# RWKV channel mix behind induced attention, one core: stage B's maxima one step sooner, and the second batch's first block transposed on TensorE in the head

## The chip, the cores and the metric

The kernel runs on one core of a Trainium2 chip. The metric is the device time of one execution in microseconds (us). Engines are named as the profile has them: PE is TensorE's matmuls, PEld its weight loads, DVE is VectorE, ACT is ScalarE, POOL is GpSimd, and SPq is the DMA queue that SyncE feeds.

## The reference

x has 4 batches of 12608 tokens with 128 features; 32 inducing rows are given. The output of an induced attention goes through an RWKV channel mix:

```python
def mab(q, kv):
    s = scale * (q @ kv.transpose(0, 2, 1))
    s = s - s.max(-1, keepdims=True)
    a = np.exp(s)
    a /= a.sum(-1, keepdims=True) + 1e-09
    return a @ kv
h = mab(I, x)               # (4, 32, 128)
y = mab(x, h)               # (4, 12608, 128)
...
xk = mu_k * y + (1.0 - mu_k) * y_prev
xr = mu_r * y + (1.0 - mu_r) * y_prev
k = np.maximum(xk @ w_k, 0.0)     # w_k 128 x 1024
v = k * k @ w_v                   # w_v 1024 x 128
r = 1.0 / (1.0 + np.exp(-(xr @ w_r)))
return r * v
```

y_prev is y one token earlier (zero before the first). The weights arrive as 64-bit floats and are converted on the chip; all arithmetic is 32-bit.

## The kernel before, in words

**What is computed in place of the reference's steps.** A row of y is a mix of the 32 rows of h, so y is never formed. Stage A makes h of a batch, by blocks: scores of a block against the inducing rows (L391), running maximum (L394 to L414), exponentials, sums, and h accumulated (L458, L473). Stage B makes the softmax weights a of each token over the 32 rows of h, by blocks. The up projection then multiplies a tile R with tiles W0 and W1, which hold h times mu times w_k (and, in 128 columns more, w_r) for the token and for the token before. R has 128 rows: 32 rows of a in four copies, high and low parts in turn, so that W's high and low parts meet them in one matmul of 128 rows. The shift of one token is a shift of R's columns.

**Tiling.** A block is 2048 tokens (6 in a batch, and a tail of 320), a group is 512 tokens (25 in a batch, the last of 320), and a group has four units of 256 of the 1024 hidden columns. That makes 400 units, and the program is a loop of steps n, one for each unit. In step n, in this order:

- up(n): for two halves of 128 columns the matmuls L839 (R shifted forward, W0) and L841 (R, W1) into a PSUM tile ps_a, of which there are two;
- the events entered for this step by `soon`;
- in the second unit of a group, the gate's two matmuls L828 and L829, and the sigmoid L831 on ScalarE;
- the square: relu on VectorE (L851, called relu(n) here), the rounded square kh on ScalarE (L856), the full square on ScalarE (L857), and the rest kl = square - kh on GpSimd (L859). In the steps of the set `high_vector`, two in each block of 12 steps, kh is made on VectorE instead (L853, called kh(n)), which reads ps_a once more;
- down(n - 4): 6 matmuls L870, kh with w_v's high part, kh with its low part, kl with its high part;
- the events entered for this step by `at`.

When a group's last down projection is done, the gate product L875 and the transpose L886 follow on VectorE, and after every second group four stores L894 on SyncE's queue.

**What sets the order.** Every engine runs its instructions in the order in which the program issues them, and the order is written out by hand: `at(n, f)` and `soon(n, f)` put f into step n. Between the units stand, in segments of 12 steps (one block), stage A of the next batch and stage B of the next block of this one. With s the first step of a segment:

- stage A of batch b+1, `stage_a`: four transposes L359 on VectorE (`btr`) at s-3, s-1, s and s+3, each pair written to DRAM (L362, xd) and read back regrouped into xt (L365, `regroup`: two at s+1, two at s+5); the load of a later block (`load_x`, L207, 1 MB, and L200 for a tail) at s+5 behind the regroups; scores at s+13 and its maximum L394; the running maximum at s+14 (L403 to L414); exponentials at s+15; h at s+19; the accumulation L473 at s+20;
- stage B of block j+1, `stage_b`, at s+1 (the step in which stage A of the segment before has its scores): scores L649 into the PSUM tile pb_b; at the next step the transpose L656 and the maximum L659 (`trans`, `maxi`); then the subtraction L662 (`sub`), the exponential L666 on ScalarE, sum and reciprocal (L670 to L674), product and transpose back (L677, L683), high part L689 and low part L693, and the copies into R (L702, `spread`) by SyncE's queue.

All DMAs of these stages, the loads of x and the stores go through SyncE's one queue.

**The ends.** `head()` makes stage A of batch 0 (in four pieces u, v, w and the tail), converts the weights and starts W; `spin(n)` issues matmuls that only occupy TensorE. `hfin` (L528 to L550) turns h into hT and the factors h4k0, h4r0 and so on, h times mu. `start()` makes the first block of stage B in pieces (`sc`, `tu`, `df`, `ex`, `nm`, `hi`, `lo`, `put`: scores, transpose and maximum, difference L762, exponential L767, normalisation L774 to L777, high, low, copies into R L801 and L803), and W: `wpart` gives a product (L560), a high part (L563) and a low part (L566) for each of W0 and W1 and each of the two halves of the hidden columns (wa, wb) and the gate's columns (wg). The gate's first matmuls stand in step 4.

## Time and profile before

| | us |
|---|---|
| median of 3 runs | 1113.23 (1113.17 to 1113.67) |
| the profiled execution | 1114.14 |
| its span | 1111.9 |
| TensorE busy | 1088.7 |
| ScalarE busy | 966.5 |
| GpSimd busy | 951.7 |
| VectorE busy | 907.3 |

The span runs from the first to the last recorded instruction. Busy time counts instructions at work; a matmul's end is modelled, so an interval between two starts says more than a row's length. In the waits a row reads "engine, what waited, its line <- engine, what it waited for, its line: total us, count, longest". In a timeline a row has its start, its length, engine, line, operation, output <- input, tile and count, and in brackets the idle time ahead of it and what ended it. In windows a row has the stretch, its length, the busy us of PE, PEld, DVE, ACT and POOL with counts, the granted clock of TensorE, the DMA engines' busy share, and GB/s.

### The profile page before, as it was taken

The page shows a single profiled execution, that of the slowest core. Times are in us where ns is not written, and L with a number is a line of the kernel's source. Part 1 is how long each engine was busy: PE and PEld are TensorE (multiplying, and loading weights), DVE is VectorE, ACT ScalarE, POOL GpSimd, SP SyncE. Part 2 cuts the span into 40 slices and gives each one's busy share as a digit, 9 for nine tenths or more (in the row PEclk, how much of TensorE's full clock was granted, in tenths as well). Part 3 has the DMA queues.
Part 4 walks back from the last instruction along what each step waited for, and adds up shares of the span by engine and source line. Part 5 has one row for each costly group of instructions (what it writes and reads, how often), then busy time and mean ns, then how long its engine had stood idle before and what let it go on. Part 6 is the DMA issues. An engine that isn't in the chain of part 4 may idle for free.

```text
span 1111.9 us, 17188 instructions
## 1 busy us (share of the span) xinstructions
PE 1088.7 (98%) x5723; PEld 832.8 (75%) x5723; DVE 907.3 (82%) x1287; ACT 966.5 (87%) x1098; POOL 951.7 (86%) x417
## 2 busy tenths in 40 slices
PE   8899999999999999999999999999999999999997
PEld 6577777777777777777787777777777787777886
DVE  6988888986878899887778888888676888887665
ACT  6698889889889888888898988979889998999995
POOL 3388998898898988889888999879898899999997
PEclk9999999999999999999999999999999999999999
DMA  9045655661356556653235646655223132232212
GB/s 343 10 127 120 171 147 145 155 167 25 62 135 150 154 148 152 146 152 82 48 78 151 167 119 149 160 138 133 41 55 73 36 66 58 55 70 57 45 29 35
DMA packets 256247, 121.10 MB, mean 109 GB/s; under 512 B 221440, under 2 KB 224672, under 8 KB 253856
## 3 DMA queue, kind: packets, MB, share of 16 engines
q1 hardware_dynamic: 255152, 119.92, 45.2%
q8 instruction: 45, 0.74, 0.3%
q14 instruction: 42, 0.34, 0.1%
q10 hardware_dynamic: 1008, 0.10, 0.1%
HBM read 46.94 MB, written 44.70 MB: 82 GB/s over the span
## 4 chain that ended last, share of the span: by engine, by line
PE 71%; DVE 13%; ACT 4%; issue 3%; DMA 2%; POOL 0%; SPq 0%; DVEq 0%; ACTq 0%; POOLq 0%
PE ps_v L870 35%; PE ps_a L839 14%; PE ps_a L841 13%; DVE k_t L851 6%; PE pb_b L649 2%; ACT kh L856 2%; DVE kh L853 2%; PE pb_a L458 2%; PE pb_a L391 2%; PE ps_v L828 2%; PE ps_v L829 2%; DMA R<-R 1%; DVE s L656 1%; DVE oT L875 1%; ACT k_t L857 1%
## 5 line engine op out<-in xcount | busy, mean ns | idle before, releaser
L859 POOL TENSOR_TENSOR kl<-k_t,kh 128x1024 fp32r<-128x1024 f32 (+1 forms) x399 | 937.3, 2384 | 122.1 <-ACT k_t L857 101.0
L851 DVE TENSOR_SCALAR k_t<-ps_a 128x1024 f32<-128x1024 f32 (+1 forms) x400 | 479.1, 1198 | 142.0 <-PE ps_a L841 115.9
L857 ACT ACTIVATE k_t<-k_t 128x1024 f32<-128x1024 f32 (+1 forms) x400 | 418.4, 1048 | 34.1 <-DVE kh L853 23.0
L856 ACT ACTIVATE kh<-k_t 128x1024 fp32r<-128x1024 f32 (+1 forms) x352 | 365.2, 1038 | 82.7 <-PE ps_v L870 41.6
L839 PE MATMUL ps_a<-R,W 128*128 128x512 f32 (+1 forms) x800 | 323.5, 405 | 8.6 <-DVE k_t L851 4.5
L841 PE MATMUL ps_a<-R,W 128*128 128x512 f32 (+1 forms) x800 | 313.5, 392 | 0.0
L870 PE MATMUL ps_v<-kh,wvh 128*128 128x512 f32 (+1 forms) x800 | 248.4, 391 | 0.0
L870 PE MATMUL ps_v<-kl,wvh 128*128 128x512 f32 (+1 forms) x800 | 247.3, 390 | 0.9 <-POOL kl L859 0.3
L870 PE MATMUL ps_v<-kh,wvl 128*128 128x512 f32 (+1 forms) x800 | 246.8, 390 | 0.0
L839 PEld LDWEIGHTS ps_a<-R,W 128*128 128x128 f32 x800 | 150.8, 188 | 76.7 <-DVE kh L853 10.6
L870 PEld LDWEIGHTS ps_v<-kl,wvh 128*128 128x128 f32 x800 | 148.1, 188 | 38.2 <-POOL kl L859 6.9
L870 PEld LDWEIGHTS ps_v<-kh,wvh 128*128 128x128 f32 x800 | 149.6, 188 | 34.2
L870 PEld LDWEIGHTS ps_v<-kh,wvl 128*128 128x128 f32 x800 | 149.6, 188 | 34.1
L841 PEld LDWEIGHTS ps_a<-R,W 128*128 128x128 f32 x800 | 150.4, 188 | 30.6 <-issue 0.2
L875 DVE TENSOR_TENSOR oT<-ps_v,rT 128x512 f32<-128x512 f32 (+1 forms) x100 | 66.6, 666 | 1.8
L886 DVE STREAM_TRANSPOSE ot<-oT 128x512 f32<-128x512 f32 x96 | 67.2, 700 | 0.0
L853 DVE SCALAR_TENSOR_TENSOR kh<-ps_a,k_t 128x1024 fp32r<-128x1024 f32 x48 | 58.8, 1224 | 5.0
L359 DVE STREAM_TRANSPOSE xs<-xb 128x512 f32<-128x512 f32 x72 | 50.0, 694 | 11.7 <-DMA xb<-in_x_dram 11.7
L831 ACT ACTIVATE rT<-ps_v 128x512 f32<-128x512 f32 (+1 forms) x99 | 57.8, 584 | 0.3
L831 ACT ACT_TABLE_LOAD x31 | 39.8, 1283 | 0.5
L828 PE MATMUL ps_v<-R,W 128*128 128x512 f32 (+1 forms) x99 | 39.1, 395 | 0.4 <-DVE oT L875 0.4
L829 PE MATMUL ps_v<-R,W 128*128 128x512 f32 (+1 forms) x99 | 38.9, 393 | 0.0
(217 smaller groups left out, 607.7 us busy)
## 6 DMA issues: line engine op xcount, KB each, us to landing
out_dram<-ot SPq DMA_DIRECT2D x184, 128.0 KB, 3.3
xb<-in_x_dram SPq DMA_DIRECT2D x18, 1024.0 KB, 6.8
xd<-xs SPq DMA_DIRECT2D x36, 512.0 KB, 3.1
xt<-xd SPq DMA_DIRECT2D x72, 256.0 KB, 4.2
R<-ah SPq DMA_DIRECT2D x184, 64.0 KB, 2.1
R<-al SPq DMA_DIRECT2D x184, 64.0 KB, 2.1
kl<-in_x_dram SPq DMA_DIRECT2D x4, 512.0 KB, 8.8
xb<-in_x_dram SPq DMA_DIRECT2D x4, 512.0 KB, 11.1
```

The costliest lines, as they stand in the source:

```text
L828: nc.tensor.matmul(out=ps[:, :w], lhsT=S.W[0][:, F:WF], rhs=R[:, 1:w + 1], start=True, stop=False)
L831: nc.scalar.activation(out=self.rT, in_=ps[:, :w], func=AF.Sigmoid)
L839: nc.tensor.matmul(out=ps[:, c, :w], lhsT=S.W[0][:, cs], rhs=R[:, 1:w + 1], start=True, stop=False)
L841: nc.tensor.matmul(out=ps[:, c, :w], lhsT=S.W[1][:, cs], rhs=R[:, 0:w], start=False, stop=True)
L851: nc.vector.tensor_scalar(out=k, in0=self.ps[:, :, :w], scalar1=0.0, scalar2=None, op0=ALU.max)
L853: nc.vector.scalar_tensor_tensor(out=kh, in0=self.ps[:, :, :w], scalar=0.0, in1=k, op0=ALU.max, op1=ALU.mult)
L856: nc.scalar.activation(out=kh, in_=k, func=AF.Square)
L857: nc.scalar.activation(out=k, in_=k, func=AF.Square)
L859: return lambda eng, a, z: eng.tensor_tensor(out=kl[:, :, a:z], in0=k[:, :, a:z], in1=kh.bitcast(F32)[:, :, a:z], op=ALU.subtract)
L870: nc.tensor.matmul(out=self.v, lhsT=wt[:, fc, :], rhs=kk[:, c, :], start=(fc == 0 and n == 0), stop=(fc == FC - 1 and n == 2))
L875: nc.vector.tensor_tensor(out=self.oT, in0=self.v, in1=self.rT, op=ALU.mult)
L886: nc.vector.transpose(out=ot[:, o:o + w], in_=self.oT)
```

## The change

**Stage B.** `trans` and `maxi` are entered for the step of the scores instead of the next, `sub` for the next. In the variant for a batch's very first stages (`quick`) the same, and the sums, the product and the copies one step later. In stage A the first transpose moves from s-3 to s-2 and the accumulation from s+20 to s+21.

In VectorE's order around one block's stage-A maximum (step 29 and the steps behind it; mx is stage A's maximum, s stage B's transposed scores, mkr the running maximum, k_t a unit's relu) there stood before:

```order
L394 TENSOR_REDUCE mx_1539<-pb_a 128x1
L851 TENSOR_SCALAR k_t<-ps_a 128x1024
L403 TENSOR_SCALAR mh<-mx_1539 64x1
L406 TENSOR_SCALAR mkr<-mh,mkr 32x1
L413 COPY mkr<-mkr 32x1
L414 COPY mkr<-mkr 64x1
L656 STREAM_TRANSPOSE s_1580<-pb_b 128x512
L659 TENSOR_REDUCE pb_b<-s_1580 128x16
L851 TENSOR_SCALAR k_t<-ps_a 128x1024
L359 STREAM_TRANSPOSE xs<-xb 128x512
L662 TENSOR_TENSOR s_1580<-s_1580,pb_b 128x512
L875 TENSOR_TENSOR oT<-ps_v,rT 128x512
```

and now (L664, L667 and L670 are the transpose, the maximum and the subtraction, L859 the relu):

```order
L402 TENSOR_REDUCE mx_1540<-pb_a 128x1
L664 STREAM_TRANSPOSE s_1553<-pb_b 128x512
L667 TENSOR_REDUCE pb_b<-s_1553 128x16
L859 TENSOR_SCALAR k_t<-ps_a 128x1024
L411 TENSOR_SCALAR mh<-mx_1540 64x1
L414 TENSOR_SCALAR mkr<-mh,mkr 32x1
L421 COPY mkr<-mkr 32x1
L422 COPY mkr<-mkr 64x1
L670 TENSOR_TENSOR s_1553<-s_1553,pb_b 128x512
L859 TENSOR_SCALAR k_t<-ps_a 128x1024
L364 STREAM_TRANSPOSE xs<-xb 128x512
L883 TENSOR_TENSOR oT<-ps_v,rT 128x512
```

The transpose and the maximum stand ahead of the first relu, and the subtraction ahead of the second.

**Loads and stores.** `load_x` is entered ahead of the regroups of its step, and the stores of a pair of groups are sent two steps after the transpose (`send`), but for the last two groups of all. On SyncE's queue at the first load of another batch (xd and xt are the two sides of the regrouping, xb and xl the loads, R<-R a single column carried on) there stood before:

```order
L362 DMA xd<-xs 128x1024
L894 DMA out_dram<-ot 32x32x32 x4
L365 DMA xt<-xd 32x4x512 x2
L207 DMA xb<-in_x_dram 128x2048
L200 DMA xl<-in_x_dram 80x4x128
L628 DMA R<-R 128x1
```

and now:

```order
L367 DMA xd<-xs 128x1024
L212 DMA xb<-in_x_dram 128x2048
L205 DMA xl<-in_x_dram 80x4x128
L370 DMA xt<-xd 32x4x512 x2
L905 DMA out_dram<-ot 32x32x32 x4
L636 DMA R<-R 128x1
```

The load has moved past four stores and two regroups.

**Batch 1's first block.** `ahead_of_time()` is new. Sixteen transposes on TensorE in the head take the place of seven spin matmuls; four copies on ScalarE put the result into the two W tiles of batch 1, which are still free; the scores are made in step 2, copied to SBUF in step 3, and two transfers inside SBUF bring the block home to xt. The four transposes L359, the transfers by xd, and the scores in step 17 are gone for this block.

**The start.** The split of w_v into high and low parts moves from the head to behind the second piece's exponential; the later steps of w_r's conversion move between the first pieces; the gate's factors h4r are made on GpSimd from SBUF, h4k0 is made from SBUF; the gate's weights are multiplied in step 2 instead of 1, and their high and low parts made in step 3 instead of 1. In VectorE's order in the first steps (W with 64x128 are the gate's low parts, the rows behind s and pb_b the third piece of stage B) there stood before:

```order
L851 TENSOR_SCALAR k_t<-ps_a 128x1024
L359 STREAM_TRANSPOSE xs<-xb 128x512
L566 TENSOR_TENSOR W_677<-ps_v,W_677 64x128
L566 TENSOR_TENSOR W_678<-ps_v,W_678 64x128
L851 TENSOR_SCALAR k_t<-ps_a 128x1024
L756 STREAM_TRANSPOSE s_811<-pb_b 128x256
L757 TENSOR_REDUCE pb_b<-s_811 128x8
L762 TENSOR_TENSOR s_811<-s_811,pb_b 128x256
L851 TENSOR_SCALAR k_t<-ps_a 128x1024
L359 STREAM_TRANSPOSE xs<-xb 128x512
L774 TENSOR_REDUCE pb_b<-s_811 128x8
```

and now:

```order
L859 TENSOR_SCALAR k_t<-ps_a 128x1024 x2
L764 STREAM_TRANSPOSE s_823<-pb_b 128x256
L765 TENSOR_REDUCE pb_b<-s_823 128x8
L770 TENSOR_TENSOR s_823<-s_823,pb_b 128x256
L859 TENSOR_SCALAR k_t<-ps_a 128x1024
L782 TENSOR_REDUCE pb_b<-s_823 128x8
L783 TENSOR_SCALAR sm_842<-pb_b 128x8
L784 RECIPROCAL pb_b<-sm_842 128x8
L785 TENSOR_TENSOR pb_b<-s_823,pb_b 128x256
L574 TENSOR_TENSOR W_683<-ps_v,W_683 64x128
L574 TENSOR_TENSOR W_684<-ps_v,W_684 64x128
```

The gate's low parts now stand behind the third piece's normalisation, and the transposes of batch 1 are gone.

**The end.** The last unit's kl, which VectorE makes, is issued two steps later, behind the gate and the transpose of the group before the last.

The diff, cut to what the text speaks of:

```diff
         def scores():
-            ps = pb_tile("a")
+            if sooner:
+                ps = S.s1
+            else:
+                ps = pb_tile("a")
             L["s1"] = ps
-            for i in range(Q):
+            for i in range(0 if sooner else Q):
                 nc.tensor.matmul(out=ps[M * i:M * (i + 1), :], lhsT=indT, rhs=S.xt[j, i],
...
-        for c in range(Q):
-            at(t + (-3, -1, 0, 3)[c], lambda c=c: btr(c))
+        k = order_a.index((b, j))
+        for bn, jn in order_a[k + 1:]:
+            if jn < NBLK - 1:
+                at(t + 5, lambda: load_x(bn, jn))
+                if jn == NBLK - 2:
+                    at(t + 5, lambda: load_x(bn, jt))
+                break
+        for c in range(0 if sooner else Q):
+            at(t + (-2, -1, 0, 3)[c], lambda c=c: btr(c))
             at(t + (1, 1, 5, 5)[c], lambda c=c: regroup(c))
...
         at(t + 19, t_hmm)
-        at(t + 20, acc)
-        k = order_a.index((b, j))
-        for bn, jn in order_a[k + 1:]:
-            if jn < NBLK - 1:
-                at(t + 5, lambda: load_x(bn, jn))
-                if jn == NBLK - 2:
-                    at(t + 5, lambda: load_x(bn, jt))
-                break
+        at(t + 21, acc)
...
                     h4 = L["h4"][nm] = sm.tile([P, P], F32, name="h4" + nm, bufs=1)
-                    nc.scalar.activation(out=h4, in_=L["hp"], func=AF.Copy, scale=mu)
+                    nc.gpsimd.tensor_tensor(out=h4, in0=L["h"], in1=mu.broadcast_to([P, P]), op=ALU.mult)
                 else:
...
             S.hT = h[:, :M]
-            L["hp"] = ps[:, :P]
+            L["hp"], L["h"] = ps[:, :P], h
             L["h4"] = {}
...
                 h4 = L["h4"]["k0"] = sm.tile([P, P], F32, name="h4k0", bufs=1)
-                nc.scalar.activation(out=h4, in_=L["hp"], func=AF.Copy, scale=muk)
+                nc.scalar.activation(out=h4, in_=h, func=AF.Copy, scale=muk)
             else:
...
             at(t, scores)
-            for n, f in ((1, trans), (1, maxi), (1, sub), (2, total), (2, recip), (3, mult), (3, back), (4, low)):
+            for n, f in ((0, trans), (0, maxi), (1, sub), (3, total), (3, recip), (4, mult), (4, back), (5, low)):
                 at(t + n, f)
             soon(t + 2, expo)
-            soon(t + 4, high)
+            soon(t + 5, high)
             for i in range(Q):
-                at(t + 5 + i, lambda i=i: spread(i))
+                at(t + 6 + i, lambda i=i: spread(i))
             return
         at(t, scores)
-        at(t + 1, trans)
-        at(t + 1, maxi)
-        at(t + 2, sub)
+        at(t, trans)
+        at(t, maxi)
+        at(t + 1, sub)
         at(t + 3, expo)
...
                 dst = out[self.b, t0:t0 + o - o0 + w, :].rearrange("(s q) (j d) -> j q s d", q=M, d=M)
-                for i in range(Q):
-                    eng = nc.scalar if self.b == B - 1 and g == NG - 1 and i % 2 else nc.sync
-                    eng.dma_start(out=dst[i], in_=ot[M * i:M * (i + 1), o0:o + w]
-                                      .rearrange("q (s d) -> q s d", d=M))
+                final = self.b == B - 1 and g == NG - 1
+                def send():
+                    for i in range(Q):
+                        eng = nc.scalar if final and i % 2 else nc.sync
+                        eng.dma_start(out=dst[i], in_=ot[M * i:M * (i + 1), o0:o + w]
+                                          .rearrange("q (s d) -> q s d", d=M))
+                if self.b == B - 1 and g >= NG - 2:
+                    send()
+                else:
+                    at(n + 2, send)
...
+    def ahead_of_time():
+        S = batches[1]
+        T = [wp.tile([P, WF], F32, name=f"W{s}")[:, :2 * G].rearrange("c (i g) -> c i g", i=2) for s in range(2)]
+        X = {"n": 0, "ps": {}}
+        for i in range(Q):
+            S.xt[0, i] = T[i // 2][:, i % 2]
+        def turn(n):
+            for _ in range(n):
+                k = X["n"]
+                X["n"] += 1
+                h, s = divmod(k, 2 * Q)
+                if s == 0:
+                    X["ps"][h] = pa.tile([P, 2, G], F32, name="ps_a")
+                nc.tensor.transpose(out=X["ps"][h][:, s // Q, (s % Q) * P:(s % Q + 1) * P],
+                                    in_=S.xb[0][:, k, :], identity=ident)
+        def keep(h, k):
+            src = X["ps"][h].rearrange("c a n -> c (a n)").rearrange("c (s i q) -> c i s q", i=Q, q=M)
+            nc.scalar.copy(out=T[k][:, :, h * G // 2:(h + 1) * G // 2].rearrange("c i (s q) -> c i s q", q=M),
+                           in_=src[:, 2 * k:2 * k + 2])
+        def scores():
+            X["s"] = pv.tile([P, G], F32, name="ps_v")
+            for i in range(Q):
+                nc.tensor.matmul(out=X["s"][M * i:M * (i + 1), :], lhsT=indT, rhs=S.xt[0, i],
+                                 start=True, stop=True)
+        def settle():
+            S.s1 = st.tile([P, G], F32, name="e1t", bufs=1)
+            nc.scalar.copy(out=S.s1, in_=X["s"])
+        def home():
+            S.xtb[0] = xt_pool.tile([P, Q, G], F32, name="xt")
+            for k in range(2):
+                nc.sync.dma_start(out=S.xtb[0][:, 2 * k:2 * k + 2, :], in_=T[k])
+            for i in range(Q):
+                S.xt[0, i] = S.xtb[0][:, i, :]
+        return turn, keep, scores, settle, home
+    sooner = ahead_of_time()
     def head():
...
         S = batches[0]
+        turn, keep = sooner[:2]
         work = [conv["k", 0], conv["k", 1], conv["v", 0], conv["v", 1], []]
...
         w.expo()
-        for c in range(FC // cg):
-            split_wv(c)
-        spin(5)
+        turn(10)
+        keep(0, 0)
+        keep(0, 1)
         v.etrans()
...
         weights()
+        turn(2)
         w.hmm(1)
         w.acc()
-        run(conv["r", 0][:2])
-        spin(2)
+        turn(4)
+        keep(1, 0)
+        keep(1, 1)
         hfin()
...
         S = batches[0]
-        run([gates, sc0, sc1, tu0, df0, ex0, wa[0][0], wa[1][0], wb[0][0], lambda: spin(2), tu1, nm0, *conv["r", 0][2:], wa[0][1], hi0,
-             wa[1][1], wb[0][1], lo0, wa[0][2], put0, lambda: spin(2),
-             df1, ex1, wa[1][2], nm1, hi1])
-        for n, f in ((0, wb[1][0]), (0, wb[1][1]), (1, lambda: run([w[0] for w in wg])),
-                     (1, sc2), (1, put1)):
+        whigh, wlow = zip(*[split_wv(c) for c in range(FC // cg)])
+        scores_1, settle_1, home_1 = sooner[2:]
+        rexp, rman, rsign, rjoin = conv["r", 0]
+        run([sc0, gates, rexp, sc1, tu0, df0, ex0, wa[0][0], wa[1][0], wb[0][0], lambda: spin(2), tu1, nm0, wa[0][1],
+             hi0, rman, rsign, wa[1][1], wb[0][1], lo0, put0, lambda: spin(2), wa[0][2], wa[1][2], df1, rjoin, ex1,
+             *whigh, *wlow, nm1, hi1])
+        for n, f in ((0, wb[1][0]), (0, wb[1][1]), (1, sc2), (1, put1), (2, lambda: run([w[0] for w in wg])), (2, scores_1)):
             soon(n, f)
-        for n, f in ((0, lo1), (0, wb[0][2]), (0, wb[1][2]), (2, tu2), (2, df2), (2, ex2), (3, nm2)):
+        for n, f in ((0, wb[0][2]), (0, wb[1][2]), (0, lo1),
+                     (2, tu2), (2, df2), (2, ex2), (3, nm2)):
             at(n, f)
         for prod, high, low in wg:
-            soon(1, high)
-            at(1, low)
+            soon(3, high)
+            at(3, low)
+        at(3, settle_1)
+        at(3, home_1)
         for k, (high, low, put) in enumerate(pl1):
...
                 low = grp.square(u, n in high_vector)
-                low(nc.vector if n == end else nc.gpsimd, 0, grp.w)
+                if n < end:
+                    low(nc.gpsimd, 0, grp.w)
             if 1 <= m <= len(units) and units[m - 1][1] == NU - 1:
-                units[m - 1][0].store()
+                units[m - 1][0].store(n)
+            if n == end + 2:
+                low(nc.vector, 0, units[end][0].w)
             if old is not None:
```

More of the change, by code (lines that the diff above doesn't have):

```diff
@@ L168, in split_wv, with high, low @@
         cs = slice(c * cg, (c + 1) * cg)
-        nc.scalar.copy(out=wvh[:, cs, :], in_=wv_sb[:, cs, :])
-        nc.gpsimd.tensor_tensor(out=wvl[:, cs, :], in0=wv_sb[:, cs, :], in1=wvh.bitcast(F32)[:, cs, :],
-                                op=ALU.subtract)
+        def high():
+            nc.scalar.copy(out=wvh[:, cs, :], in_=wv_sb[:, cs, :])
+        def low():
+            nc.gpsimd.tensor_tensor(out=wvl[:, cs, :], in0=wv_sb[:, cs, :], in1=wvh.bitcast(F32)[:, cs, :],
+                                    op=ALU.subtract)
+        return high, low
     def groups(j):
@@ L348, in stage_a @@
         tw = TAIL // Q
-        last = 4 if tail else 0
+        sooner = b == 1 and j == 0
         def btr(c):
@@ L416, in expo @@
         def expo():
-            e1t = st.tile([P, G], F32, name="e1t", bufs=1)
+            e1t = S.s1 if sooner else st.tile([P, G], F32, name="e1t", bufs=1)
             if j == 0:
@@ L875, in gate, with store @@
             nc.vector.tensor_tensor(out=self.oT, in0=self.v, in1=self.rT, op=ALU.mult)
-        def store(self):
+        def store(self, n):
             g, w = self.g, self.w
```

## The prediction

> **What bounds the kernel now.** I read the busy shares first, then the waits, then TensorE's and VectorE's timelines around the waits that repeat. In the busy shares each engine has its busy us, its share of the span and its instructions:
>
> ```profile
> span 1111.9 us, 17188 instructions
> PE 1088.7 (98%) x5723; PEld 832.8 (75%) x5723; DVE 907.3 (82%) x1287; ACT 966.5 (87%) x1098; POOL 951.7 (86%) x417
> ```
>
> TensorE bounds: 98% busy. The change removes hardly any matmul, so what can be won is time in which TensorE stands still or starts late, and a gain elsewhere that ends no such wait counts nothing. The view of waits gives, for each group, total us, count and longest:
>
> ```profile
> PEld ps_a L839 <- DVE kh L853: 10.6, 16, 0.8
> ```
>
> Sixteen weight loads of an up projection wait for the rounded square on VectorE. One of them in TensorE's timeline (start, length; the bracket is idle time with modelled ends, so I go by distances of starts):
>
> ```profile
> 92.38 1.06 PE L391 MATMUL pb_a<-xt,indT 128*32 128x512 f32 x8
> 93.27 1.04 PE L649 MATMUL pb_b<-xt,hT 128*32 128x512 f32 x8
> ...
> 98.51 0.62 PE L870 MATMUL ps_v<-kl,wvh 128*128 128x512 f32 x2
> 98.96 0.40 PE L839 MATMUL ps_a<-R,W 128*128 128x512 f32 x1
> 99.19 0.41 PE L841 MATMUL ps_a<-R,W 128*128 128x512 f32 x1
> ...
> 103.63 0.62 PE L870 MATMUL ps_v<-kl,wvh 128*128 128x512 f32 x2
> 104.50 0.49 PE L839 MATMUL ps_a<-R,W 128*128 128x512 f32 x1 [0.24 <-DVE kh L853]
> 104.83 0.39 PE L841 MATMUL ps_a<-R,W 128*128 128x512 f32 x1
> ```
>
> Up(20) follows the last pair of its predecessor by 98.96 − 98.51 = 0.45 us and its second matmul by 0.23. Up(22) follows by 0.87 and 0.33. The place loses 0.42 + 0.10 = 0.52 us. On VectorE, up to there:
>
> ```profile
> 93.52 0.69 DVE L394 TENSOR_REDUCE mx<-pb_a 128x1 f32<-128x512 f32 x1 [0.96 <-PE pb_a L391]
> 95.55 1.22 DVE L851 TENSOR_SCALAR k_t<-ps_a 128x1024 f32<-128x1024 f32 x1 [1.34 <-PE ps_a L841]
> ...
> 97.62 0.72 DVE L656 STREAM_TRANSPOSE s<-pb_b 128x512 f32<-128x512 f32 x1
> 98.37 0.69 DVE L659 TENSOR_REDUCE pb_b<-s 128x16 f32<-128x512 f32 x1
> 98.98 1.21 DVE L851 TENSOR_SCALAR k_t<-ps_a 128x1024 f32<-128x1024 f32 x1
> ...
> 100.73 0.65 DVE L662 TENSOR_TENSOR s<-s,pb_b 128x512 f32<-128x512 f32 x1
> ...
> 103.22 1.22 DVE L853 SCALAR_TENSOR_TENSOR kh<-ps_a,k_t 128x1024 fp32r<-128x1024 f32 x1
> ```
>
> VectorE idles 1.34 us at step 18 and is late five instructions later: from 95.55 on it runs almost without a gap to kh's end at 104.44, just ahead of the delayed matmul.
>
> **Part 1, stage B's maxima.** Transpose and maxima (L656, L659) go ahead of relu(18). Their scores end at 93.27 + 1.04 = 94.31; the pair takes 98.98 − 97.62 = 1.36, so relu(18) starts at about 95.75 where it started at 95.55: 0.2 to 0.3 later. From behind it 1.36 us vanish. So kh(20) ends at about 104.44 − 1.36 + 0.25 = 103.35, or, with starts rounded up on the way, 103.65. Undelayed, up(22) wants it at 103.63 + 0.45 = 104.08. So 0.4 to 0.7 us are to spare and the 0.52 goes away. Going through TensorE's timeline I count this wait, at this place of a block, 14 times (the other two of the 16 stand in the start and at a late load): 14 × 0.52 = **−7.3 us**. Next late is nothing: relu(18) must have left its PSUM tile by up(20) at 98.96 and ends at 97.05, 1.9 early. The last stage of batch 0 has a related wait, on VectorE for the exponentials, and TensorE behind it:
>
> ```profile
> 298.85 0.69 DVE L670 TENSOR_REDUCE pb_b<-s 128x16 f32<-128x512 f32 x1 [0.83 <-ACT s L666]
> ```
> ```profile
> 299.87 0.40 PE L841 MATMUL ps_a<-R,W 128*128 128x512 f32 x1
> 300.69 0.50 PE L828 MATMUL ps_v<-R,W 128*128 128x512 f32 x1 [0.42 <-DVE oT L875]
> ```
>
> The subtraction comes a step sooner and so do the exponentials' inputs: 0.82 − 0.23 + 0.10, **−0.7 us**; between 0 and that, since the exponentials' own place on ScalarE is unchanged.
>
> **Part 2, the load ahead of the regroups.** On SyncE's queue at a new batch, and what waited:
>
> ```profile
> 458.77 0.34 SPq L362 DMA_DIRECT2D xd<-xs  x1
> 464.15 3.89 SPq L894 DMA_DIRECT2D out_dram<-ot  x4
> 469.30 0.38 SPq L207 DMA_DIRECT2D xb<-in_x_dram  x1
> ```
> ```profile
> 477.91 0.71 DVE L359 STREAM_TRANSPOSE xs<-xb 128x512 f32<-128x512 f32 x1 [3.31 <-DMA xb<-in_x_dram]
> ```
> ```profile
> 477.62 0.62 PE L870 MATMUL ps_v<-kl,wvh 128*128 128x512 f32 x2
> 479.79 0.50 PE L839 MATMUL ps_a<-R,W 128*128 128x512 f32 x1 [1.54 <-DVE k_t L851]
> ```
>
> The transpose needs a load that was issued behind the stores. TensorE loses 2.17 − 0.45 = 1.72. In the new order the load follows xd directly, so issue moves from 469.30 to about 460, and the block's first transpose stands one step later. The wait was 3.31 and the move is 9 us: it goes entirely. The other late load, one batch on, costs about 1.3 by the same reading; with 0.1 each for the following matmul, **−3.1 us** (at least −2, if stores two steps later delay something else by some tenths).
>
> **Part 3, the start.** Batch 1's first block is transposed on TensorE in place of spin matmuls, so its scores leave step 17: the eight L391 above took 93.27 − 92.38 = 0.89. Against this stands the gate's weights. Before:
>
> ```profile
> 54.67 0.40 PE L828 MATMUL pb_a<-R,W 128*128 128x512 f32 x1
> ```
> ```profile
> 55.60 0.40 ACT L767 ACTIVATE s<-s 128x256 f32<-128x256 f32 x1
> ```
> ```profile
> 56.47 0.39 DVE L774 TENSOR_REDUCE pb_b<-s 128x8 f32<-128x256 f32 x1
> 57.34 0.43 DVE L777 TENSOR_TENSOR pb_b<-s,pb_b 128x256 f32<-128x256 f32 x1
> ```
>
> Now the gate's low weights stand on VectorE behind the third piece's normalisation, and that behind the exponential, which is itself behind the squares. From 56.00 the normalisation takes 57.77 − 56.47 = 1.30, the two lows a quarter each by their size: the gate matmul at 57.4 to 57.7 instead of 54.67, **+2.7**. What was waiting just behind in the batch is then no longer late:
>
> ```profile
> 71.88 0.50 PE L839 MATMUL ps_a<-R,W 128*128 128x512 f32 x1
> 77.24 0.47 PE L839 MATMUL ps_a<-R,W 128*128 128x512 f32 x1 [0.43 <-DVE k_t L851]
> ```
>
> These two are late by 0.3 and 0.6 by their distances, and the transposes of batch 1 that VectorE ran there are gone. With 0.9 from step 17 and 0.2 to 0.5 from up(0) starting sooner (its converters and the gate factors leave the chain ahead), 2.7 − 0.9 − 0.9 − 0.4 = **+0.5**, bounds −1.0 (up(0) a whole microsecond sooner, with the gate behind it) and +2.5 (nothing repaid but some tenths). The four copies run on ScalarE while TensorE still has spin or weight work, and the two transfers inside the chip are wanted only in step 23: nothing. The split of w_v, moved behind the first piece of stage B, is first read by down(0), which stands behind the same delayed gate matmul: nothing; if it is later than that, down(0) is late by the difference.
>
> **Part 4, the end.** VectorE's last instructions and SyncE's last issue:
>
> ```profile
> 1102.47 2.10 DVE L859 TENSOR_TENSOR kl<-k_t,kh 128x640 fp32r<-128x640 f32 x1 [1.64 <-ACT k_t L857]
> 1104.49 0.68 DVE L875 TENSOR_TENSOR oT<-ps_v,rT 128x512 f32<-128x512 f32 x1
> 1106.02 0.49 DVE L875 TENSOR_TENSOR oT<-ps_v,rT 128x320 f32<-128x320 f32 x1
> ```
> ```profile
> 1107.99 1.10 SPq L894 DMA_DIRECT2D out_dram<-aT  x2
> ```
>
> The gate of group 23 and its transpose (0.68 + 0.7) fit into the 1.64 before kl. The last gate then waits for the last matmul, and the stores of group 23 are out of the way of the last: **−1.2**, bounds −0.4 (only the last gate moves) and −1.6.
>
> **Sum.** −7.3 − 0.7 − 3.1 + 0.5 − 1.2 = −11.8. The profiled execution took 1114.14 us, 0.91 above the median of the runs shown; on that median 1113.23 − 11.8 = **1101.4 us**.
>
> **The clock as a rule against part 3.** The last matmul, and the granted clock behind it (the fraction stands last but two):
>
> ```profile
> 1104.93 0.45 PE L870 MATMUL ps_v<-kl,wvh 128*128 128x320 f32 x2
> ```
> ```profile
> 1108.00:1109.00 1.00, 0.00 (x0) 0.00 (x0) 0.00 (x0) 0.00 (x0) 0.00 (x0) 0.83 0.99 142
> 1109.00:1111.00 2.00, 0.00 (x0) 0.00 (x0) 0.00 (x0) 0.00 (x0) 0.00 (x0) 0.50 0.51 71
> ```
>
> The mean of 0.83 puts the fall to 0.50 at two thirds of that microsecond, 3.3 us after the last matmul's end. The idle time ahead of the delayed gate matmul is up to 57.7 − 54.7 = 3.0 us, close to it. The Trainium skill, TensorE: Matmul & The Clock Gate, part 1, says the same: after about 3.4 us of idle window the clock is halved until a window as long has been busy, with windows that run free. This trace agrees at its end; whether the start crosses the line no row of before can show.
>
> **Rivals.**
> - *The maxima start late.* If the pair begins only when up(18) shows (95.55 rather than 94.31), everything behind moves by 0.9 to 1.2, the spare 0.4 to 0.7 is used up and the −7.3 is lost: 1101.4 + 7.3 = 1108.7. For it: the scores' PSUM bank is freed by other engines. Against: VectorE was idle there for 1.34. Chance 0.12.
> - *The start goes cold.* If TensorE's gap reaches 3.3 us, the next 3.3 us or so run at 0.50 and do half their work: +1.7, and the gap itself up to +0.6: about 1103.6. Chance 0.08.
> - *The early load pushes the regroups.* The load took 477.91 − 469.30 = 8.6 us from issue to use; regroups behind it land that much later. They are needed four steps on at the shortest block, some 10 us by steps of 2.3 to 3.2; three such blocks at 0 to 1.5 us: about 1104. Chance 0.04.
> - *VectorE blocks in order, slower than before.* Now relu(18) stands behind an instruction that needs the stage's scores. If these are late by d, relu(18) is too, and beyond 1.9 us up(20) is: 24 blocks × (d − 1.9) on top of 1108.7, so slower than before from d = 2.1 on; at 2.5, 1123. Against: the scores' inputs were loaded blocks before. Chance 0.04.
>
> **How the numbers follow.** The forecast keeps 0.72. Its bounds: all best, 1101.4 − 1.5 − 0.4 − 0.9 = 1098.6, less some tenths if small waits shrink too; all worst, 1101.4 + 2.0 + 0.8 + 1.1 + 0.7 = 1106. With the first rival in, the range is 1097.5 to 1109. A measurement of this kernel can tell about 0.2%, 2.2 us, from no change. Faster by more: 0.91; within: 0.05 (the first rival with the worst start and end); slower: 0.04.
>
> **What would show it.** Right: no wait of L839's load for VectorE's kh in the blocks of batches 0 to 2; kh(20)'s end 0.4 or more ahead of up(22); no DVE wait for a load; step 17 shorter by 0.9; the gate's first matmul near 57.5. Wrong: a wait of VectorE at the moved transposes, up projections waiting for relu at two steps' distance, or a granted clock under 1.00 after step 4.

## The result, and the profile after

| | us |
|---|---|
| before, median of 4 runs | 1113.45 (1113.17 to 1114.73) |
| changed, median of 4 runs | 1104.96 (1103.39 to 1105.28) |
| ratio | 0.9919, interval 0.9902 to 0.9936 |
| the changed kernel's profiled execution | 1105.28, span 1103.2 |

The change makes the kernel 8.5 us faster, 3.3 us less than forecast; the time is 3.6 us over the forecast 1101.4. One execution of a later run (`no_maxima`) took 1520.14 us at a mean granted clock of 0.654 and is left out of what follows. On the changed kernel's page the first two lines are

```profile
span 1103.2 us, 17165 instructions
PE 1083.8 (98%) x5725; PEld 837.3 (76%) x5725; DVE 908.7 (82%) x1283; ACT 969.9 (88%) x1101; POOL 952.3 (86%) x419
```

TensorE still bounds. Laying the first matmuls of the 400 up projections of both profiled executions side by side gives the length of each step before and after, and so an account of the whole span. The lines are sums over steps; a matmul that follows a wait at some 0.1 more is counted with it.

| where | forecast | measured |
|---|---|---|
| 14 places where up waited for kh | -7.3 | -7.4 |
| late loads, steps 159 and 259 | -3.1 | -3.2 |
| end of batch 0, step 93 | -0.7 | -0.7 |
| the start, up to and with step 18 | +0.5 | +3.4 |
| the end, behind the last up projection | -1.2 | -0.4 |
| down projections that waited for GpSimd's kl, seven steps | "some tenths" | -2.2 |
| other small waits, steps 27, 135, 277 and the rest | none | -1.1 |
| tail blocks, steps 73, 169, 269 | none | +2.0 |
| step 96 | none | +0.9 |
| sum of the spans' difference | -11.8 | -8.7 |

The row on down projections rests on the weight loads that wait for GpSimd, before and after:

```profile
PEld ps_v L870 <- POOL kl L859: 6.9, 20, 0.6
PEld ps_v L878 <- POOL kl L867: 1.5, 3, 0.6
```

The waits for kh at the 14 places are gone. Of the 16 one is left, in step 13, which the change made longer (below):

```profile
PEld ps_a L847 <- DVE kh L861: 0.8, 1, 0.8
```

In the timeline of VectorE and then of TensorE, at the place that the prediction showed (everything stands some 3.4 us later, from the start):

```profile
105.51 1.23 DVE L861 SCALAR_TENSOR_TENSOR kh<-ps_a,k_t 128x1024 fp32r<-128x1024 f32 x1
```
```profile
107.09 0.62 PE L878 MATMUL ps_v<-kl,wvh 128*128 128x512 f32 x2
107.55 0.40 PE L847 MATMUL ps_a<-R,W 128*128 128x512 f32 x1
107.79 0.40 PE L849 MATMUL ps_a<-R,W 128*128 128x512 f32 x1
```

kh(20) ends at 106.74 and up(22) starts 0.46 behind the last pair, with its second matmul 0.24 behind. The room is 0.8 us, where 0.4 to 0.7 was forecast.

The start went another way. TensorE's timeline, VectorE's, and the windows (the granted clock stands last but two):

```profile
55.22 0.40 PE L849 MATMUL ps_a<-R,W 128*128 128x512 f32 x1
57.93 0.49 PE L836 MATMUL pb_a<-R,W 128*128 128x512 f32 x1 [2.31 <-DVE W L574]
58.26 0.46 PE L837 MATMUL pb_a<-R,W 128*128 128x512 f32 x1
```
```profile
57.12 0.43 DVE L785 TENSOR_TENSOR pb_b<-s,pb_b 128x256 f32<-128x256 f32 x1
57.58 0.50 DVE L574 TENSOR_TENSOR W<-ps_v,W 64x128 fp32r<-64x128 f32 x2
```
```profile
57.00:58.00 1.00, 0.07 (x1) 0.07 (x1) 0.93 (x4) 0.97 (x2) 1.00 (x1) 1.00 0.67 279
58.00:59.00 1.00, 1.00 (x4) 0.78 (x5) 0.97 (x2) 1.00 (x3) 1.00 (x2) 0.77 0.02 8
59.00:60.00 1.00, 1.00 (x4) 0.81 (x3) 0.75 (x3) 0.98 (x4) 1.00 (x1) 0.50 0.00 0
60.00:61.00 1.00, 1.00 (x4) 0.80 (x3) 0.35 (x2) 0.99 (x2) 0.99 (x1) 0.50 0.00 0
61.00:62.00 1.00, 1.00 (x4) 0.73 (x3) 0.00 (x0) 1.00 (x2) 0.00 (x0) 0.53 0.00 0
62.00:63.00 1.00, 1.00 (x6) 0.82 (x5) 0.31 (x1) 0.97 (x2) 0.00 (x0) 1.00 0.00 0
```

The gate's first matmul stands at 57.93, close to the 57.4 to 57.7 forecast. By the shares of the first and last of these windows the clock fell at 58.54, when the gate's matmuls were already running, and was full again at 61.94: 3.4 us at half, which is the rival "the start goes cold". It is not in every execution: three of the four took 1104.95 to 1105.28 with a mean clock of 0.996 or 0.997, the fourth 1103.39 with 0.998.

Two waits are new that the prediction hadn't. At a tail block (step 73, step 74 starts behind it), VectorE and TensorE:

```profile
247.76 0.70 DVE L894 STREAM_TRANSPOSE ot<-oT 128x512 f32<-128x512 f32 x1
248.39 0.30 DVE L481 SCALAR_TENSOR_TENSOR acc<-acc,alpha,pb_a 128x128 f32<-128x128 f32 x1
```
```profile
248.80 1.06 PE L399 MATMUL pb_a<-xt,indT 128*32 128x512 f32 x8 [0.58 <-PE ps_v L878]
```

and at step 96, where VectorE stands 2.52 us:

```profile
305.48 1.20 DVE L859 TENSOR_SCALAR k_t<-ps_a 128x1024 f32<-128x1024 f32 x1
309.20 0.69 DVE L701 TENSOR_TENSOR al<-pb_b,ah 128x512 fp32r<-128x512 f32 x1 [2.52 <-ACT ah L697]
309.81 1.22 DVE L859 TENSOR_SCALAR k_t<-ps_a 128x1024 f32<-128x1024 f32 x1
```
```profile
311.08 0.41 PE L847 MATMUL ps_a<-R,W 128*128 128x320 f32 x1 [0.70 <-DVE R L634]
```

The profile puts the wait of the tail's scores down to a TensorE matmul that had ended at 248.21, 0.58 us earlier; the accumulation that ends at 248.69 is what reads pb_a last. Both readings were tried.

### The profile page after: what moved, and what is told of

Its sections match the earlier page's. It is cut to its first block, busy times and chain, and to the rows that moved or that the text cites. A ratio compares the mean times of both kernels' runs of the same rounds, so it can differ in the third digit from the quotient of the medians.

```text
span 1103.2 us, 17165 instructions
## 1 busy us (share of the span) xinstructions
PE 1083.8 (98%) x5725; PEld 837.3 (76%) x5725; DVE 908.7 (82%) x1283; ACT 969.9 (88%) x1101; POOL 952.3 (86%) x419
## 4 chain that ended last, share of the span: by engine, by line
PE 91%; DVE 4%; ACT 2%; issue 1%; DMA 1%; POOL 1%; POOLq 0%; SPq 0%; DVEq 0%; ACTq 0%
PE ps_v L878 47%; PE ps_a L847 17%; PE ps_a L849 16%; PE ps_v L836 2%; PE ps_v L837 2%; PE pb_b L657 2%; PE pb_a L466 2%; PE pb_a L399 2%; ACT kh L864 1%; POOL kl L867 1%; DMA xl<-in_x_dram 1%; DVE k_t L859 0%; DMA xt<-W 0%; DVE mx L263 0%; PE pb_a L586 0%
## 5 line engine op out<-in xcount | busy, mean ns | idle before, releaser
L859 DVE TENSOR_SCALAR k_t<-ps_a 128x1024 f32<-128x1024 f32 (+1 forms) x400 | 480.4, 1201 | 122.0 <-PE ps_a L849 109.2
L364 DVE STREAM_TRANSPOSE xs<-xb 128x512 f32<-128x512 f32 x68 | 47.5, 699 | 0.0
```

What stands on the lines that cost most here:

```text
L859: nc.vector.tensor_scalar(out=k, in0=self.ps[:, :, :w], scalar1=0.0, scalar2=None, op0=ALU.max)
```

## The experiments

Each run is the changed kernel with the edit shown, but for the last of the loads. Runs that were made together share their runs of the kernel before.

### The start: the gap, the clock, the whole

Only the place of the gate's weights:

```diff
-        ..., (1, sc2), (1, put1), (2, lambda: run([w[0] for w in wg])), (2, scores_1)):
+        ..., (1, lambda: run([w[0] for w in wg])), (1, sc2), (1, put1), (2, scores_1)):
...
-            soon(3, high)
-            at(3, low)
+            soon(1, high)
+            at(1, low)
```

> The changed kernel, with the gate's weights multiplied and split at step 1 as before the change, ahead of the third piece's normalisation. Theory 1 (the gap of 2.5 us ahead of the gate's first matmul comes from the low parts' place on VectorE, and the granted clock falls because of that gap): the first gate matmul stands near 55 instead of 57.93, no stretch after it has a granted clock under 1.00, step 4 falls from 6.57 to about 2.9; some of it comes back at step 3 as a wait for relu: 1101 to 1102.5. Theory 2 (the high parts on ScalarE, behind the squares, are late as well): the gate matmul stays after 57 and the time at 1104 to 1105. If the clock's fall has another cause than the gap, 8 matmuls at 0.42 us distance are there all the same.

Measured: 1102.48 us (1102.33 to 1102.64), ratio to before 0.9893 (0.9874 to 0.9912). Step 4 fell from 6.57 to 2.88, and from 55 to 63 us no window shows a clock under 1.00. TensorE's timeline:

```profile
55.06 0.40 PE L836 MATMUL pb_a<-R,W 128*128 128x512 f32 x1
```

Theory 1 holds. Of 4.15 us won up to step 4, 0.9 came back at once: the gate of step 5 waits 1.20 for the ScalarE copy of batch 1's first scores, which holds its PSUM tile; another 0.8 came back at step 13.

The same gap, filled:

```diff
+        soon(4, lambda: spin(20, pb_tile("a").rearrange("p (a n) -> p a n", a=2)))
         soon(4, lambda: units[0][0].zgate(first=True))
```

> The changed kernel with 20 more spin matmuls (their result is not used) just ahead of the gate's first matmuls, which fill most of TensorE's gap there. Theory 1 (the fall of the granted clock comes from the gap): the gate matmul stays at about 57.9, the clock stays at 1.00 behind it, step 4 falls from 6.57 to about 5.4 and step 5 from 3.19 to 2.8: about 1.6 us faster, 1103.3. Theory 2 (the slow matmuls have another cause, such as copies or transfers beside them): 8 matmuls at 0.42 us distance stay, and the time at 1105.

Measured: 1105.64 us (1105.43 to 1105.92), ratio 0.9923 (0.9907 to 0.9939). The windows:

```profile
57.00:59.00 2.00, 2.00 (x21) 2.00 (x19) 1.93 (x4) 1.97 (x4) 2.00 (x2) 1.00 0.26 107
59.00:61.00 2.00, 1.94 (x13) 1.61 (x12) 0.98 (x3) 1.97 (x4) 1.89 (x1) 1.00 0.00 0
```

The clock stays at 1.00 with the same copies and transfers beside it, so the fall comes from the gap. The expected time was missed by a mistake of size: a spin is two matmuls in the records, 40 in all in 4.62 us, so they ran to 59.94 and pushed the gate's matmul from 57.93 to 60.00. All four executions had a clock of 0.998 or more and lay within 0.5 us.

Head and start as before the change, the rest as changed (batch 1's first block through VectorE and DRAM again; the diff's hunks on `ahead_of_time`, `head`, `start`, `split_wv`, `hfin`, and `sooner` undone):

> The changed kernel with head and start as before the change: no transposes of batch 1 on TensorE, its first block through VectorE and DRAM, the split of w_v, w_r's conversion and the gate's weights in their old places. Theory 1 (the new start costs 3.46 us up to step 18, net of what it saves in steps 9, 11 and 17): 1104.96 - 3.5 = about 1101.5. Theory 2 (what it costs at the start is repaid behind step 18, since VectorE has less to do): 1104 or more.

Measured: 1102.86 us (1102.61 to 1102.97), ratio 0.9896 (0.9873 to 0.9919). It is 2.1 us faster than the changed kernel: theory 1, with a smaller sum (2.3 us up to step 18 by the step lengths). Up to step 12 it is 4.3 us ahead, then gives 1.1 back at step 13, whose wait grows, and 0.9 at step 17. The wait of step 13 isn't the new start's, then.

### The accumulation ahead of the tail

```diff
-        at(t + 21, acc)
+        at(t + (20 if j == NBLK - 3 else 21), acc)
```

> The changed kernel, with the accumulation of stage A's block ahead of the tail one step earlier again (s+20); everything else as changed. Theory 1 (the tail's scores wait for their PSUM tile, which the accumulation on VectorE gives back only in the same step): steps 73, 169 and 269 lose their 0.65 us each and last 3.88 as before; 1104.96 - 1.95 = about 1103.0. Theory 2 (the load that now goes ahead delays the regrouped block): the three steps stay at 4.53 and the time stays at 1105.

Measured: 1102.40 us (1101.54 to 1103.29), ratio 0.9892 (0.9872 to 0.9913). VectorE, then TensorE, at step 73:

```profile
246.50 0.34 DVE L481 SCALAR_TENSOR_TENSOR acc<-acc,alpha,pb_a 128x128 f32<-128x128 f32 x1
```
```profile
248.01 1.06 PE L399 MATMUL pb_a<-xt,indT 128*32 128x512 f32 x8
```

The three steps are at 3.87 to 3.90 again. Loads and regroups stood as in the changed kernel, so theory 2 falls. Two of the four executions took 1101.5 to 1101.7 (clock 0.998 and more) and two 1103.1 to 1103.3 (0.996 and 0.997): the gap at the start is still there.

### Stage B's maxima

The hunk on `stage_b` undone, both variants:

> The changed kernel with stage B's transpose, maximum and subtraction (and the quick variant) in their old steps. Theory 1 (the 14 waits of up(s+6) for kh, and the wait at the end of batch 0, went because of this part): they are back at 0.28 to 0.53 each plus 0.68: +6.0 + 0.7, less 0.87 at step 96 that the quick variant caused: about 1110.5 to 1111. Theory 2 (they went because loads and stores moved, or VectorE has fewer transposes): 1105 to 1106.

Measured: 1114.1 us (1112.67 to 1114.9, nine executions), ratio 0.9997 (0.9986 to 1.0008). Without this part nothing is left of the gain. The waits are back:

```profile
PEld ps_a L847 <- DVE kh L861: 9.8, 15, 0.8
```

Step by step it loses 0.27 to 0.51 at each of the 14 places, 0.68 at step 93, and gains 0.85 and 0.87 at steps 13 and 96. Theory 1 holds. That it costs 9.2 and not some 6 has two main grounds that the expectation left out: the 0.1 behind each wait, 1.5 in all, and the down projections of steps 98, 99, 109, 198, 199, 209 and 298, which wait for kl again, together 2.1 (with relu later on VectorE, GpSimd's subtraction probably is too).

### The quick variant's later steps

```diff
-            for n, f in (..., (3, total), (3, recip), (4, mult), (4, back), (5, low)):
+            for n, f in (..., (2, total), (2, recip), (3, mult), (3, back), (4, low)):
...
-            soon(t + 5, high)
+            soon(t + 4, high)
...
-                at(t + 6 + i, lambda i=i: spread(i))
+                at(t + 5 + i, lambda i=i: spread(i))
```

> The changed kernel with the later steps of the quick variant (sums, product, high and low parts, copies) in their old steps; transpose, maximum and subtraction stay early. Theory 1 (in the later place VectorE's low part stands at the head of its queue and waits 1.9 to 2.5 us for ScalarE's high part, and gate and relu behind it are late): step 13 falls from 3.66 to about 2.8 and step 96 from 2.84 to 1.97; up to 0.4 may come back at step 11: about 1103.5. Theory 2 (it is the early transposes of the quick variant that delay these steps): both steps stay.

Measured: 1104.17 us (1103.25 to 1105.08), ratio 0.9907 (0.989 to 0.9925). Two executions took 1105.0 and two 1103.3, like the changed kernel's with and without the clock's fall. Steps 13 and 96 are free as theory 1 has it, 2.81 and 1.97. But step 93 lost the same 0.87, and steps 98 and 99 lost 0.8. VectorE and TensorE at step 93:

```profile
299.80 0.69 DVE L678 TENSOR_REDUCE pb_b<-s 128x16 f32<-128x512 f32 x1 [2.05 <-ACT s L674]
```
```profile
301.64 0.49 PE L836 MATMUL ps_v<-R,W 128*128 128x512 f32 x1 [0.59 <-DVE oT L883]
```

So the earlier subtraction alone does not free step 93: here it is early, and the sum waits for the exponential all the same. The wait stands at the sum, so what freed the step is taken to be the sum's later place; the other steps of the variant moved with it, and whether the later sum would do without the earlier subtraction was not run. By the step lengths the later places are worth about nothing in all: what they win at steps 93, 98 and 99 they lose at 13 and 96.

### The loads

Load and stores in their old order:

```diff
-        k = order_a.index((b, j))
-        for bn, jn in order_a[k + 1:]:
-            ...
         for c in range(0 if sooner else Q):
...
         at(t + 21, acc)
+        k = order_a.index((b, j))
+        for bn, jn in order_a[k + 1:]:
+            ...
...
-                if self.b == B - 1 and g >= NG - 2:
-                    send()
-                else:
-                    at(n + 2, send)
+                send()
```

> The changed kernel with the load behind the regroups and the stores sent at once, as before the change. Theory 1 (only the late loads of steps 159 and 259 hang on this part): waits of 1.7 and 1.3 us are back there, or 0.5 less each since the first transpose stands a step later; steps 73, 169 and 269 keep their 0.65; 1107 to 1108. Theory 2 (the early load pushed the tail's regroups): the three steps go back to 3.88, and the sum is 1105 to 1106.

Measured: 1104.21 us (1104.14 to 1104.87), ratio 0.9912 (0.9894 to 0.993). Neither theory: no wait came back at steps 159 and 259, and the tail's 0.65 stayed. Then the first transpose of a block moved back as well,

```diff
-            at(t + (-2, -1, 0, 3)[c], lambda c=c: btr(c))
+            at(t + (-3, -1, 0, 3)[c], lambda c=c: btr(c))
```

first on top of the old loads:

> The changed kernel with the load behind the regroups, the stores at once, and in addition the first transpose of a block at s-3 again, as before the change. Theory 1 (it was the first transpose's place, one step later, that ended the waits for the late loads, and the load's new place alone wasn't needed): steps 159 and 259 wait again, 1.7 and 1.3 us, and the time is about 3 us over the run with old loads alone: 1107. Theory 2 (the loads come sooner by the time the rest has won, and wait nowhere): no wait, 1104.2.

Measured: 1103.57 us (1102.3 to 1104.22), ratio 0.9903 (0.9888 to 0.9918). No wait again, so theory 1 falls. SyncE's queue and VectorE at the load of step 157:

```profile
465.46 0.38 SPq L212 DMA_DIRECT2D xb<-in_x_dram  x1
```
```profile
473.11 0.71 DVE L364 STREAM_TRANSPOSE xs<-xb 128x512 f32<-128x512 f32 x1 [1.84 <-DMA R<-R]
```

The load is still late: VectorE stands 1.84 us where it stood 3.31. (The row names the copy R<-R, but the load, 7.6 us under way, landed at 473.06, just ahead of the transpose.) Counted from step 155's first matmul, the load goes out 1.0 us and lands 2.0 us sooner than in the kernel before, and TensorE no longer waits. Which part of the rest of the change does this was not separated; the early maxima are the likeliest. Then with only the transpose moved back:

> The changed kernel with only the first transpose at s-3 again; loads go ahead of the regroups and stores two steps later, as changed. Theory 1 (the load's new place by itself is enough, as the forecast had it: issue some 8 us sooner): no wait at steps 159 and 259, 1105. Theory 2 (the load lands late in both orders and only the transpose's place counts): waits of 1.3 to 1.7 us at both, 1108.

Measured: 1104.88 us (1104.66 to 1105.3), ratio 0.9917 (0.9902 to 0.9931): no wait, as theory 1 has it. Last, the kernel before with nothing but the two edits on loads and stores:

> The kernel before the change with only this part of it: the load goes ahead of the regroups, and stores are sent two steps later. Theory 1 (the load's new place is enough by itself, and the early maxima are enough by themselves; the two don't add): the waits of steps 159 and 259 go, 3.1 us faster than before, about 1110.5; the 14 waits for kh stay. Theory 2 (only the moved maxima, through earlier stores and more room on VectorE, ended these waits): both stay and the time is within 0.5 us of before.

Measured: 1110.41 us (1110.06 to 1110.83), ratio 0.9974 (0.9964 to 0.9983). Steps 159 and 259 lost 1.71 and 1.28, steps 27, 135 and 277 another 0.7, and the waits for kh stayed:

```profile
PEld ps_a L839 <- DVE kh L853: 10.5, 16, 0.8
```

The load's new place is enough by itself, as theory 1 has it, and so, by `old_loads_old_btr`, is the rest of the change; that the early maxima alone would do, no run shows. In the changed kernel the two do the same work, and the load's place adds nothing.

The new order costs something at the end. In the changed kernel's waits of SyncE's queue, from 1097 to 1103 us:

```profile
SPq L905 <- DVE aT L894: 1.6, 1, 1.6
SPq L905 <- DMA out_dram<-aT: 1.6, 1, 1.6
```

The last store on SyncE's queue waits 1.6 us until a store of ScalarE's queue has landed. With the old places of the stores it follows its predecessor by 0.36 (1097.81 and 1098.17), and from the last up projection to the end of the span it is 11.25 us instead of 12.34. The semaphore events of the trace show that in the changed kernel the two stores share one completion counter, which both queues use in turn; in `old_loads` the last four stores have one each. So the new order of loads and stores moved the two onto the same one; which of the two moves did it was not separated. In the medians the old order is worth 0.75 us (`old_loads` against the changed kernel) and 1.3 us (`old_loads_old_btr` against `old_btr`).

### What mends it

The three mended places at once (`acc_early`, `gate_early`, `quick_old`), and the copy of batch 1's first scores ahead of unit 3's square:

```diff
-        at(3, settle_1)
+        soon(3, settle_1)
```

> The changed kernel with four edits at once: the accumulation ahead of the tail one step earlier, the gate's weights at step 1, the quick variant's later steps as before, and the copy of batch 1's first scores ahead of unit 3's square on ScalarE (so that the PSUM tile it holds is free for the gate of step 5). Theory 1 (each wait is by itself): from the changed kernel -1.95, -3.25 up to step 6, about -1.2 at step 5, -0.85 and -0.87 at steps 13 and 96: 1104.96 - 8.1 = about 1097. Theory 2 (the start's time is set by one chain, which only moves the wait to the next matmul): 1100 to 1101.

Measured: 1100.42 us (1100.33 to 1100.66), ratio 0.9877 (0.9861 to 0.9892). Steps 4, 5, 13, 73, 96, 169 and 269 are free. Step 6 gave back 0.9 and step 11 0.8, so theory 2 has part of it; step 93 gave back 0.9 and steps 98 and 99 0.8 together, as in `quick_old`.

The second version has the same edits, but keeps the sums late and puts the low part a step behind the high one; the last four stores go on one queue (shown against the changed kernel):

```diff
-            for n, f in (..., (3, total), (3, recip), (4, mult), (4, back), (5, low)):
+            for n, f in (..., (3, total), (3, recip), (4, mult), (4, back), (6, low)):
...
-                at(t + 6 + i, lambda i=i: spread(i))
+                at(t + 7 + i, lambda i=i: spread(i))
...
-                        eng = nc.scalar if final and i % 2 else nc.sync
+                        eng = nc.sync
```

> The kernel with the four mended places, but with the quick variant's sums and product in their new steps, its low part a step behind the high part (t+6) and the copies at t+7; and the last four stores all on SyncE's queue. Theory 1 (the low part alone, at the head of VectorE's queue, made the waits of steps 13 and 96, and the later sums are what ended those of steps 93, 98 and 99; the last store waited 1.6 us for the store of ScalarE's queue): steps 11, 13, 93, 96, 98 and 99 are all free, 2.6 us under all_mended, and 0.2 to 0.6 less at the end: 1097 to 1098. Theory 2 (the copies into R come too late now, or VectorE's total work sets these steps): a wait of up projections 100 to 103 or of step 13 stays, 1099 to 1100.

Measured: 1097.63 us (1097.08 to 1098.5), ratio to before 0.9854 (0.9837 to 0.987), 7.3 us under the changed kernel. VectorE at the end of batch 0:

```profile
303.56 0.69 DVE L701 TENSOR_TENSOR al<-pb_b,ah 128x512 fp32r<-128x512 f32 x1 [0.85 <-ACT ah L697]
```

The low part still waits for ScalarE, 0.85 instead of 2.52, and TensorE doesn't see it: steps 11, 13, 93, 96 and 98 are free, step 99 keeps 0.4, and step 6 the 0.9 of the first version. Theory 1. The end is 0.4 shorter than the changed kernel's.

## Why the prediction was right, and where it was not

The time lies in the range partly by luck. What the sum missed cost 6.6 us (the start 2.9, the tails 2.0, step 96 0.9, the end 0.8); gains that stood in no term, the waits for kl and other small waits, gave 3.3 back.

- **Part 1, the 14 places: right**, in mechanism and size; `no_maxima` brings each back. What fell short is the sum around it: the waits for GpSimd's kl at seven steps shrank by 2.2 us, and `no_maxima` brings these back too. The prediction had this as "some tenths".
- **The end of batch 0: right size by luck, wrong cause.** The step that failed is "the subtraction comes a step sooner and so do the exponentials' inputs". The exponential's place on ScalarE didn't move, and `quick_old`, with the subtraction early, has the whole wait. The wait stands at the reader of the exponential, the sum, and the changed kernel has that a step later.
- **Part 2, the late loads: right size, half the cause.** The step "the wait was 3.31 and the move is 9 us: it goes entirely" is true by itself (`loads_alone`). But it was added to the rest as though independent, and the rest of the change ends the same wait without it (`old_loads_old_btr`). As measured the edit adds nothing to the changed kernel, and it takes 1.1 us of the span at the end.
- **Part 3, the start: the mechanism right, the sum wrong by 2.9.** The gate's matmul came at 57.93, 3.3 later than before where the term had 2.7, and what was to be repaid at steps 9, 11 and 17 was: 0.3, 0.6 and 0.9. Failed: "up(0) starting sooner", which brought 0.15, while up(4) was 0.85 later (the third piece's scores wait for a low part that now stands behind two W lows, and up(2) follows them); the clock, which was a rival with a chance of 0.08 and cost 1.6 in most executions (`spin_gap`, `gate_early`; why its line of 3.3 us was too high stands in the last section); and step 13's 0.85, from the quick variant's low part, for which no term stood.
- **Part 4, the end: right where it was reasoned, given back elsewhere.** The last gate follows the last matmul, and the stores of group 23 went early. The last store didn't, because of the completion counter. With the old places of the stores the end is 1.5 us shorter than before; forecast was 1.2.
- **Not in the sum: an accumulation and a low part.** Front and diff name both moves (s+20 to s+21; the quick variant's steps), and neither was priced. They cost 2.0 us at the tails and 1.7 at steps 13 and 96. The rival for an instruction that blocks VectorE's queue named the right mechanism at the wrong place: it was the low part waiting for ScalarE, not the maxima waiting for the scores.
- **The rival "the early load pushes the regroups" was false**: the tails' 0.65 has the look of it, and `acc_early` shows that it is the accumulation.

## What to carry to other kernels

When an edit moves ten things by a step, price every one that reads or frees a shared tile: the accumulation, moved by one step, cost 2.0 us, more than the 1.2 that the end's whole term was meant to win. Two edits that end the same wait don't add; before summing, ask of each wait which of the edits alone would end it. On an engine that runs in order, the reader of another engine's result belongs a step behind it, for all that is queued behind the reader waits too.

## What the runs showed of the hardware

- The granted clock fell to 0.50 after TensorE had stood still for 2.3 us by the records (2.7 between starts, 55.22 to 57.93), not only behind the last matmul as in the kernel before. It lasted 3.4 us and cost 1.6 us. By their times 3 of 4 executions of the changed kernel have it, 2 of 4 of `acc_early` and of `quick_old`, all 4 of `old_loads` and of `old_btr`, and none of 4 of `gate_early`, in which there is no such gap. The gap before it, in the same execution, did no harm:

```profile
49.93 0.64 PE L756 MATMUL pb_b<-xt,hT 128*32 128x128 f32 x16 [1.60 <-DVE al L803]
```

- In these traces the falls go by TensorE's busy time in fixed stretches of 3.41 us, not by the length of a gap alone. Within each profile the clock's changes stand whole multiples of 3.41 us apart (in the changed kernel's 58.53, 61.95 and 1099.60: one of them, then 304). Cut into such stretches from there, all 14 profiles agree: while the clock is full, it falls behind every stretch in which the records have TensorE busy for 1.78 us or less, and behind none with 1.81 or more. In the changed kernel's windows the first stretch holds the gap of 1.60, the second most of the gap of 2.31, and the third is the one at half:

```profile
48.29:51.70 3.41, 1.81 (x24) 1.45 (x24) 2.68 (x4) 2.44 (x4) 2.39 (x2) 1.00 0.02 5
55.12:58.53 3.41, 1.09 (x5) 0.54 (x4) 2.97 (x8) 3.38 (x7) 3.41 (x2) 1.00 0.67 275
58.53:61.95 3.42, 3.42 (x10) 2.67 (x9) 1.56 (x3) 3.39 (x7) 2.46 (x2) 0.50 0.00 0
```

Where the stretches lie differs from execution to execution. A gap of 2.31 us does no harm where the end of a stretch splits it into two parts that both stay under 1.6; estimated from 2.31 and 3.41 that is about one case in four, and 9 of the 33 executions of the seven kernels with this gap went without the fall. So the prediction's 3.3 us behind the last matmul was one value of many: in `old_start` the clock fell 1.3 us behind it (1094.77 and 1096.08), in `all_mended_2` 4.5 (1089.52 and 1094.01).

- Stores on two queues can wait for one another by a completion counter that they share: 1.6 us for the last store of the changed kernel.
